# Four converted weight units parked in DRAM after their first use, instead of converted a second time

## The chip, the cores and the metric

The kernel runs on one core of a Trainium2 chip. The metric is device time in microseconds of one execution, as the median of three runs. TensorE (PE) multiplies matrices, PEld loads its weights, VectorE (DVE), ScalarE (ACT) and GpSimd (POOL) do the elementwise work, and SyncE (SP) issues nearly all the transfers, in order, on one queue. TensorE has a granted clock, which the profile prints as a share of full speed.

## The reference, cut to what matters

```
x = attention(rope(q), rope(k), v)        # 2 batches x 8 heads, 576 rows of 64 -> x: 1152 tokens x 512
h = x @ w_in                              # 512 -> 2048      w_in, w_out are float64
g = max(0.01 * h, h)
x1 = (g @ w_out).astype(float32)          # 2048 -> 512
# then a mixture of 8 experts, top 2 of 8 per token:
for e: out[rows of e] += gate * (relu(x1[rows of e] @ w1[e]) @ w2[e])
```

Only the middle part, `x1`, has weights in double precision. Everything else is float32.

## The kernel before, in words

The kernel has three stages: attention (to about 180 us of the span), the dense feed-forward layer (to about 400 us) and the experts.

Every product is made in split precision: a float32 value is written as a high part and a low part, each in a type that TensorE multiplies at full rate, and three products (high-high, low-high, high-low) are added. So each weight has to be converted before TensorE can use it.

**Units and slots.** The 2048 hidden features are 16 units of 128. A unit has two parts, its slice of `w_in` (part 0) and of `w_out` (part 1), 0.5 MB of float64 each. Its converted form is two tiles of 128x2x512 (`hi`, `lo`), 0.5 MB each, in one of `NSLOT` = 12 slots (line 143). The list `units` (lines 149, 150) runs c = 0..15 for the 16 dense units, c = 16..19 for the first four of them again, and c = 20 on for the expert units. Unit c lives in slot c % 12, so c = 12..15 overwrite units 0..3, and 16..19 overwrite 4..7. Slots 1 and 2 share their memory with the last set of q and k of the attention stage (`set_q`, `set_k`).

**Two passes.** The dense layer handles the first 768 tokens in one pass over c = 0..15 (lines 641 to 649) and the last 384 in `dense2` (line 662) over c = 4..19: the twelve units that are still in slots, and then the four that have been overwritten.

**Conversion of a dense part** (`convert`, line 179) is a chain of six stages on 128x512 elements: ACT takes the absolute value (0), DVE clamps (1), shifts and takes in the sign (2, two instructions), takes in the low word (3), ACT writes `hi` (4), DVE writes `lo` (5). Part p = 2c or 2c + 1. An expert part is float32 and needs stages 4 and 5 only. `load_part` (line 153) brings a raw part into one of three buffers.

**Order.** PE, ACT, DVE and POOL run their instructions in the order in which the program writes them. In attention that order is a string of letters; in the dense layer `leaky` (line 588), called once per step, weaves its own activation (`g_t`, `g_f`, `g_h`, `g_l`), the conversion stages of parts p - 1, p, p + 1, and the hooks, which hold the routing of the first 768 tokens and the copies of `x1` rows to DRAM (`rows`, line 715). `dense2` converts parts 32 on, two per unit. The transfers are put in order on SP's queue by a scheduler, which works from the dependences.

**Closing a head pair.** In attention the softmax sums of each pair go to DRAM (`inv_sums`, line 464), come back to all partitions (`inv_sum`, line 470), POOL multiplies (line 474) and ACT writes `xh` (line 486). All these transfers are on SP's queue.

Of the kernel before, what the change touches and what calls it, by code (L numbers as in the profile page):

```python
# [10 lines left out]
F32 = mybir.dt.float32  # L11
# [66 lines left out]
def f32(t):  # L78
    return t.bitcast(F32)
# [3 lines left out]
def fused_kernel(ctx, tc, q, k, v, w_in, w_out, w_gate, w_noise, noise, w1, w2, consts, out):  # L83
    nc = tc.nc
    V, A, G, T = nc.vector, nc.scalar, nc.gpsimd, nc.tensor

    def pool(name, bufs=1, **kw):
        return tc.tile_pool(name=name, bufs=bufs, reuse_waits="tile", **kw)
# [9 lines left out]
    dpool = ctx.enter_context(pool("scratch", space=DRAM))  # L98
# [44 lines left out]
    NSLOT = 12  # L143
    slots = [[epool.tile([128, 2, 512], F32R, name=f"w{n}_0") for n in "hl"]]
# [5 lines left out]
    units += [("ex", e, f) for e in range(E) for f in range(8)]  # L150
    staged = {}

    def load_part(p):

        c, part = divmod(p, 2)
        if p >= last_part[0] or p in staged or (p, 0) in done:
            return
        u = units[c]
        if u[0] == "in":
            f = u[1]  # L160
            t = rpool.tile([128, 512, 2], I32, name="raw")
            if part == 0:
                nc.sync.dma_start(t.rearrange("p (k f) w -> p k (f w)", k=4),
                                  w_in.bitcast(I32)[:, f * 256:(f + 1) * 256].rearrange("(k p) f -> p k f", p=128))
            else:
                nc.sync.dma_start(t.rearrange("p d w -> p (d w)"), w_out.bitcast(I32)[f * 128:(f + 1) * 128, :])
        else:
            _, e, f = u
            t = rpool.tile([128, 512], F32, name="raw32", tag="raw")
            if part == 0:  # L170
                nc.sync.dma_start(t.rearrange("p (k f) -> p k f", k=4),
                                  w1[e, :, f * 128:(f + 1) * 128].rearrange("(k p) f -> p k f", p=128))
            else:
                nc.sync.dma_start(t, w2[e, f * 128:(f + 1) * 128, :])
        staged[p] = t

    word, done, last_part, last_conv = {}, set(), [2 * len(units)], [2 * len(units)]

    def convert(p, stage):

        c, part = divmod(p, 2)
        if not 0 <= p < last_conv[0] or (p, stage) in done:
            return
        done.add((p, stage))
        hi, lo = slots[c % NSLOT]
        if units[c][0] == "in":
            if stage == 0:
                word[p] = rpool.tile([128, 512], I32, name="word")
                A.activation(f32(word[p]), f32(staged[p][:, :, 1]), AF.Abs)
                return  # L190
            m, hw, lw = word[p], staged[p][:, :, 1], staged[p][:, :, 0]
            if stage == 1:
                V.tensor_scalar(f32(m), f32(m), 2.0 ** -15, F32_MAX_AS_HIGH_WORD, op0=OP.max, op1=OP.min)
            elif stage == 2:
                V.tensor_scalar(m, m, 3, 0x3FFFFFFF, op0=OP.logical_shift_left, op1=OP.bitwise_and)
                V.scalar_tensor_tensor(m, hw, -0x40000000, m, op0=OP.bitwise_and, op1=OP.bitwise_or)
            elif stage == 3:
                V.scalar_tensor_tensor(m, lw, 29, m, op0=OP.logical_shift_right, op1=OP.bitwise_or)
            elif stage == 4:
                A.activation(hi[:, part], f32(m), AF.Copy)  # L200
            else:
                V.tensor_tensor(lo[:, part], f32(m), f32(hi)[:, part], op=OP.subtract)
        else:
            t = staged[p]
            if stage == 4:
                A.activation(hi[:, part], t, AF.Copy)  # L206
            elif stage == 5:
                V.tensor_tensor(lo[:, part], t, f32(hi)[:, part], op=OP.subtract)  # L208
# [279 lines left out]
    def x_low(pr):  # L488
        k, parts = x_parts(pr)
        t = closing.pop(pr)[4]  # L490
        for i, there, here in parts:
# [41 lines left out]
            "t": (sums, [(pr, n) for pr in range(NP) for n in range(3)]),  # L533
            "B": (sums_in, [(pr, n) for pr in range(NP) for n in range(2)]),
            "Z": (load_small, [(i,) for i in range(7)]), "F": (load_part, [(p,) for p in range(6)])}
    for n, f in (("T", invert), ("s", sums_out), ("N", normalize), ("X", x_high), ("Y", x_low)):
        work[n] = (f, [(pr,) for pr in range(NP)])
# [4 lines left out]
    for i, n in enumerate("!#$%&*"):  # L542
        work[n] = (convert, [(p, i) for p in range(6)])
# [26 lines left out]
    def mm1(c, h, x, cols, n, lows_last=False):  # L570
        hi, lo = slots[c % NSLOT]
        terms = [(k, w, m) for k in range(4) for w, m in ((hi, x[0]), (lo, x[0]), (hi, x[1]))]
        if lows_last:
            terms.sort(key=lambda t: t[2] is x[1])
        for i, (k, w, m) in enumerate(terms):
            T.matmul(h[:, :n], w[:, 0, k * 128:(k + 1) * 128], m[:, k, cols:cols + n], start=(i == 0), stop=(i == 11))  # L576

    def mm2(c, g, y, n, first, last):

        hi, lo = slots[c % NSLOT]  # L580
        for d in range(4):
            ds = slice(d * 128, d * 128 + 128)
            b, o, opens = y[d]
            for t, (w, m) in enumerate(((hi, g[0]), (lo, g[0]), (hi, g[1]))):
                T.matmul(b[:, o:o + n], w[:, 1, ds], m[:, :n], start=(first and opens and t == 0),  # L585
                         stop=(last and t == 2), skip_group_check=True)

    def leaky(h, n, ps, hooks, group):

        t = gpool.tile([128, 512], F32, name="g_t")  # L590
        g = gpool.tile([128, 512], F32, name="g_f")
        gh = gpool.tile([128, group], F32R, name=f"g_h{group}")
        gl = gpool.tile([128, group], F32R, name=f"g_l{group}")
        for at, p in enumerate(ps):
            convert(p, 1)
            if at == 0:
                A.activation(t[:, :n], h[:, :n], AF.Copy, scale=0.01)  # L597
                V.tensor_tensor(g[:, :n], h[:, :n], t[:, :n], op=OP.max)  # L598
            if at < len(hooks):
                hook(hooks[at])  # L600
            convert(p - 1, 4)
            convert(p, 2)
            if at == 0:
                A.activation(gh[:, :n], g[:, :n], AF.Copy)
                V.tensor_tensor(gl[:, :n], g[:, :n], f32(gh)[:, :n], op=OP.subtract)  # L605
            convert(p, 3)
            convert(p - 1, 5)
            convert(p + 1, 0)
            load_part(p + 3)
        return gh, gl  # L610
# [6 lines left out]
    for p in (6, 7, 8):  # L617
        load_part(p)
# [14 lines left out]
    def step(c, o, n):  # L633
        h = hA if o == 0 else hB
        mm1(c, h, x, o, n)
        q = next(calls)
        return leaky(h, n, (6 + q,), (base + q,), NA if o == 0 else NB)
# [3 lines left out]
    for f in range(17):  # L641
        if f < 15:
            gA[f + 1] = step(f + 1, 0, NA)
        if f < 16:
            mm2(f, gA.pop(f), ya, NA, f == 0, f == 15)
        if f > 0:
            gB[f - 1] = step(f - 1, NA, NB)
        if f > 1:
            mm2(f - 2, gB.pop(f - 2), yb, NB, f == 2, False)
# [6 lines left out]
    def close_first():  # L656
        mm2(15, gB.pop(15), yb, NB, False, True)
        for n in range(2):
            e = A.copy if n else V.tensor_copy
            e(x1[0][:, 2 * n:2 * n + 2, NA:P1], bank[4 + n].rearrange("p (d n) -> p d n", d=2))  # L660

    def dense2(cs, p, at):

        x = (xh[1], xl[1])
        g = None
        for i in range(len(cs) + 1):
            if i < len(cs):
                h = bank[6 + i % 2]
                mm1(cs[i], h, x, 0, NC)
                after = leaky(h, NC, (p + 2 * i, p + 2 * i + 1), (at + 2 * i, at + 2 * i + 1), NA)  # L670
            if i == 0:
                close_first()
            else:
                mm2(cs[i - 1], g, ya, NC, i == 1, i == len(cs))
            g = after
        for d in range(4):
            (A.copy if d % 2 else V.tensor_copy)(x1[0][:, d, P1:NT], bank[d][:, :NC])
# [234 lines left out]
    last_part[0], last_conv[0] = 2 * len(units), 58  # L912
    load_part(32)
    dense2(list(range(16 - NSLOT, 16 + 16 - NSLOT)), 28, base2)
    assert not later, later.keys()

# [221 lines left out]
```

## Time and profile before

| | us |
|---|---|
| median of three runs (lowest to highest) | 676.95 (676.53 to 681.25) |
| the profiled execution | 678.88 |
| its span, first to last instruction | 677.1 |
| PE busy | 645.0 (95%) |
| DVE busy | 418.7 (62%) |
| ACT busy | 325.7 (48%) |
| POOL busy | 173.5 (26%) |

The mean granted clock is 0.981. PE is busy almost all of the span, so shares over the span say little; the stretches in which PE waits, or runs at a lower clock, are few, and the windows of 10 us show where they are. A row of the timeline is one instruction or a merged run of them: start, duration, engine, line, operation, output <- inputs, shape, count, and in brackets how long the engine stood idle before it and what ended that.

### The profile page before, as it was taken

How to read it: one execution, taken by the hardware profiler on the slowest of the kernel's cores; microseconds unless marked ns; L12 is line 12 of the kernel's file. 1: busy time of each engine (PE TensorE's matmuls, PEld its weight loads, DVE VectorE, ACT ScalarE, POOL GpSimd, SP SyncE). 2: the span in 40 equal slices, each digit the busy share in tenths (PEclk: the TensorE clock that was granted, in tenths of full speed). 3: DMA queues.
4: the chain of work that ended last, by engine and by line, in shares of the span. 5: the costliest groups of instructions: out<-in, count | busy, mean ns of one | idle time of the engine just before them, and what ended most of it. 6: DMA issues, size and time to landing. Idle time of an engine off the chain costs nothing. (4 is left out here: it accounts for less than half of the span.)

```text
span 677.1 us, 10441 instructions
## 1 busy us (share of the span) xinstructions
PE 645.0 (95%) x3658; PEld 555.9 (82%) x3659; DVE 418.7 (62%) x870; ACT 325.7 (48%) x659; POOL 173.5 (26%) x179
## 2 busy tenths in 40 slices
PE   7698999999999999999979998999999999999993
PEld 3587888888788888889769985889888888888882
DVE  8688555564179988843598654474756556574611
ACT  4454555575445544423445441454555545454511
POOL 9974767112130000000000001113224040505102
PEclk9899999999999999999998997999999999999998
DMA  6656433231147443420154433447676675858323
GB/s 173 188 166 180 116 75 76 63 80 51 36 139 263 147 124 125 125 63 1 56 163 140 133 92 80 134 134 194 155 201 162 196 171 165 215 148 204 103 31 41
DMA packets 89344, 86.51 MB, mean 128 GB/s; under 512 B 21316, under 2 KB 68615, under 8 KB 89287
## 3 DMA queue, kind: packets, MB, share of 16 engines
q1 hardware_dynamic: 84390, 74.92, 38.3%
q0 software_dynamic: 4608, 10.49, 7.7%
q8 instruction: 30, 0.49, 0.3%
q10 hardware_dynamic: 288, 0.39, 0.2%
q14 instruction: 28, 0.22, 0.1%
HBM read 69.95 MB, written 10.00 MB: 118 GB/s over the span
## 5 line engine op out<-in xcount | busy, mean ns | idle before, releaser
L208 DVE TENSOR_TENSOR wl<-raw,wh 128x512 fp32r<-128x512 f32 x108 | 72.3, 687 | 48.9 <-ACT wh L206 45.9
L999 POOL DMA_INDIRECT out<-y_row,idx x24 | 41.9, 1744 | 174.6 <-ACT y_row L991 170.3
L873 POOL DMA_INDIRECT got<-x_rows,idx x24 | 25.0, 1043 | 227.6 <-DVE gate L825 210.3
L206 ACT ACTIVATE wh<-raw 128x512 fp32r<-128x512 f32 x108 | 66.0, 629 | 32.9 <-DMA raw<-in_moe_w 32.4
L374 DVE TENSOR_REDUCE maxes<-pM 128x1 fp32r<-128x576 f32 (+1 forms) x73 | 54.1, 754 | 44.0 <-PE pM L367 43.4
L982 PE MATMUL bank<-wh,g_x 128*128 128x512 f32 x216 | 78.3, 403 | 0.6 <-ACT set_q L206 0.5
L436 PE MATMUL pO<-p,VF 128*128 128x288 f32 x256 | 72.7, 413 | 0.0
L423 ACT ACTIVATE p<-pS 128x576 f32<-128x576 f32 (+1 forms) x73 | 46.3, 649 | 53.0 <-PE pS L417 51.3
L576 PE MATMUL bank<-xe_h,wh 128*128 128x320 f32 x216 | 67.8, 314 | 0.0
L576 PE MATMUL bank<-xe_h,wl 128*128 128x320 f32 x216 | 67.7, 314 | 0.0
L576 PE MATMUL bank<-xe_l,wh 128*128 128x320 f32 x216 | 66.8, 312 | 0.0
L597 ACT ACTIVATE g_t<-bank 128x512 f32<-128x512 f32 (+2 forms) x48 | 23.5, 489 | 75.9 <-PE bank L576 75.9
L585 PE MATMUL bank<-g_l,wh 128*128 128x384 f32 (+2 forms) x152 | 52.1, 342 | 0.9 <-DVE g_l L605 0.9
L436 PEld LDWEIGHTS pO<-p,VF 128*128 128x128 f32 x256 | 45.2, 192 | 8.9 <-issue 1.1
L585 PE MATMUL bank<-g_h,wh 128*128 128x384 f32 (+2 forms) x152 | 52.4, 345 | 0.0
L576 PE MATMUL bank<-xh,wh 128*128 128x384 f32 (+2 forms) x152 | 52.1, 343 | 0.0
L576 PE MATMUL bank<-xh,wl 128*128 128x384 f32 (+2 forms) x152 | 51.9, 342 | 0.0
L576 PE MATMUL bank<-xl,wh 128*128 128x384 f32 (+2 forms) x152 | 51.8, 341 | 0.0
L585 PE MATMUL bank<-g_h,wl 128*128 128x384 f32 (+2 forms) x152 | 51.6, 339 | 0.0
L598 DVE TENSOR_TENSOR g_f<-bank,g_t 128x512 f32<-128x512 f32 (+2 forms) x48 | 26.6, 555 | 38.9 <-ACT g_t L597 38.6
L965 DVE SCALAR_TENSOR_TENSOR g_x<-bank,g_x 128x320 fp32r<-128x320 f32 x64 | 31.0, 484 | 30.1 <-ACT g_x L964 30.0
L982 PEld LDWEIGHTS bank<-wh,g_x 128*128 128x128 f32 x216 | 40.5, 188 | 8.4 <-ACT set_q L206 0.8
(238 smaller groups left out, 1530.4 us busy)
## 6 DMA issues: line engine op xcount, KB each, us to landing
raw<-in_moe_w SPq DMA_DIRECT2D x128, 256.0 KB
raw<-in_moe_w_in SPq DMA_DIRECT2D x20, 512.0 KB
raw<-in_moe_w_out SPq DMA_DIRECT2D x20, 512.0 KB
inv_sum<-inv_sums SPq DMA_DIRECT2D x16, 144.0 KB
out<-none SPq DMA_DIRECT2D x9, 256.0 KB
raw_q<-in_q SPq DMA_DIRECT2D x8, 256.0 KB
raw_k<-in_k SPq DMA_DIRECT2D x8, 256.0 KB
VF<-in_v SPq DMA_DIRECT2D x16, 128.0 KB
```

Source lines behind the costliest of these rows:

```text
L206: A.activation(hi[:, part], t, AF.Copy)
L208: V.tensor_tensor(lo[:, part], t, f32(hi)[:, part], op=OP.subtract)
L374: V.tensor_reduce(maxes[pr % 2][rows, i:i + 1], maxed.pop((pr, a, j))[rows, :, 0:288], axis=AX.XY, op=OP.max, negate=True)
L423: A.activation(t[r], scored.pop((pr, a, j))[r, :, 0:288], AF.Exp, scale=0.125)
L436: T.matmul(acc[g][:, z, 0:288], w, p[r, z, :], start=opens, stop=closes)
L576: T.matmul(h[:, :n], w[:, 0, k * 128:(k + 1) * 128], m[:, k, cols:cols + n], start=(i == 0), stop=(i == 11))
L585: T.matmul(b[:, o:o + n], w[:, 1, ds], m[:, :n], start=(first and opens and t == 0), stop=(last and t == 2), skip_group_check=True)
L598: V.tensor_tensor(g[:, :n], h[:, :n], t[:, :n], op=OP.max)
L873: G.indirect_dma_start(out=t[:n], out_offset=None, in_=x1_rows, in_offset=bass.IndirectOffsetOnAxis(ap=idx[e][:n, st:st + 1], axis=0))
L965: V.scalar_tensor_tensor(g[:, C:2 * C], h[:, :C], 0.0, f32(g)[:, :C], op0=OP.max, op1=OP.subtract)
L982: T.matmul(yr[st], s, w, start=(f == 0 and t == 0), stop=(f == 7 and t == 2))
L999: s = G.indirect_dma_start(out=out, out_offset=bass.IndirectOffsetOnAxis(ap=idx[e][:n, st:st + 1], axis=0), in_=r[:n], in_offset=None, com ...
```

## The change: four units are written out and read back

When the first pass has reached f = 3..6, the converted `hi` and `lo` of units 0..3 are written to DRAM (`keep`). In `dense2`, after the last product with unit c - 12, they are read into the slot of unit c = 16..19 (`bring`). Raw loads and conversions of c = 16..19 are left out.

```diff
+    def keep(c, w):
+        kept[c, w] = dpool.tile([128, 1024], F32, name=f"kept{c}_{w}", bufs=1)
+        nc.sync.dma_start(kept[c, w], f32(slots[c % NSLOT][w]).rearrange("p a b -> p (a b)"))
+
+    def bring(c, w):
+        nc.sync.dma_start(f32(slots[c % NSLOT][w]).rearrange("p a b -> p (a b)"), kept[c - 16, w])
     def load_part(p):
-        if p >= last_part[0] or p in staged or (p, 0) in done:
+        if p >= last_part[0] or p in staged or (p, 0) in done or 16 <= c < 32 - NSLOT:
             return
     def convert(p, stage):
-        if not 0 <= p < last_conv[0] or (p, stage) in done:
+        if not 0 <= p < last_conv[0] or (p, stage) in done or 16 <= c < 32 - NSLOT:
             return
     ...
             mm2(f, gA.pop(f), ya, NA, f == 0, f == 15)
+        if 3 <= f < 19 - NSLOT:
+            for w in range(2):
+                keep(f - 3, w)
     ...
                 mm2(cs[i - 1], g, ya, NC, i == 1, i == len(cs))
+                c = cs[i - 1] + NSLOT
+                if c < 32 - NSLOT:
+                    for w in range(2):
+                        bring(c, w)
```

The orders of PE and POOL stay as they are. DVE loses 40 instructions and ACT 16, all of them the conversion of parts 32 to 39; SP loses eight loads and gains eight stores and eight loads, and the scheduler puts them in places that the diff does not show.

On DVE, in `dense2` around the fourth to the sixth of its units (`word` is the part under conversion, `noisy`, `mx`, `ix` belong to the routing), before:

```order
L193 TENSOR_SCALAR word<-word 128x512
L598 TENSOR_TENSOR g_f<-bank_1893,g_t 128x384
L769 TENSOR_TENSOR noisy<-c,ln 128x48
...
L777 MAX_INDEX ix<-mx,noisy 128x8 x6
L195 TENSOR_SCALAR word<-word 128x512
L196 SCALAR_TENSOR_TENSOR word<-raw,word 128x512
L605 TENSOR_TENSOR g_l_3533<-g_f,g_h_3532 128x384
L198 SCALAR_TENSOR_TENSOR word<-raw,word 128x512
L202 TENSOR_TENSOR wl_1881<-word,wh_1880 128x512
```

and with the change:

```order
L608 TENSOR_TENSOR g_f<-bank_1893,g_t 128x384
L786 TENSOR_TENSOR noisy<-c,ln 128x48
...
L794 MAX_INDEX ix<-mx,noisy 128x8 x6
L615 TENSOR_TENSOR g_l_3493<-g_f,g_h_3492 128x384
L608 TENSOR_TENSOR g_f<-bank_1892,g_t 128x384
```

The activation and the routing keep their order, and the conversions between them are gone.

On SP, in attention, around the closing of the first head pair (`wh_88`, `wl_89` are slot 0; `raw<-in_moe_w_out` and `raw<-in_moe_w_in` are parts 5 and 6), before:

```order
L270 DMA raw_k_116<-in_k 128x2x256
L273 DMA raw_k_116<-in_k 64x2x64
L464 DMA inv_sums<-rc 128x9
L166 DMA raw<-in_moe_w_out 128x1024
L470 DMA inv_sum<-inv_sums 64x576 x2
L163 DMA raw<-in_moe_w_in 128x4x256
```

and with the change:

```order
L158 DMA kept_0_2187<-wh_88 128x1024
L280 DMA raw_k_116<-in_k 128x2x256
L176 DMA raw<-in_moe_w_out 128x1024
L474 DMA inv_sums<-rc 128x9
L283 DMA raw_k_116<-in_k 64x2x64
L158 DMA kept_1_2189<-wl_89 128x1024
L173 DMA raw<-in_moe_w_in 128x4x256
L480 DMA inv_sum<-inv_sums 64x576 x2
```

The two stores of unit 0 are issued here, not in the dense layer, and two loads of raw weights have moved ahead of the sums. The stores of unit 1 stand in the same way just ahead of `inv_sums` of the sixth pair, those of unit 2 behind it, and those of unit 3 at the start of the dense layer.

On SP, in `dense2`, with the change (`raw_3462`, `raw_3516`, `raw_3526`, `raw_3570` are the first four expert parts):

```order
L181 DMA raw_3462<-in_moe_w 128x4x128
L184 DMA raw_3516<-in_moe_w 128x512
L181 DMA raw_3526<-in_moe_w 128x4x128
L161 DMA wl_1877<-kept_1_2189 128x1024
...
L161 DMA wl_1883<-kept_1_2453 128x1024
L743 DMA x_rows<-x_row 128x512
L161 DMA wh_1882<-kept_0_2451 128x1024
L743 DMA x_rows<-x_row 128x512 x2
L184 DMA raw_3570<-in_moe_w 128x512
```

Before, five loads of dense parts stood between the first rows of `x1` here; now the first three expert parts come first, then the eight loads from DRAM.

## Rows read from the trace of the kernel before

**Rows 1.** Windows: busy time of each engine, granted clock, DMA share, GB/s.

```profile
210.00:220.00 10.00, 10.00 (x57) 8.71 (x56) 9.67 (x21) 5.60 (x11) 0.00 (x0) 1.00 0.76 263
340.00:350.00 10.00, 8.78 (x53) 8.46 (x52) 9.69 (x22) 5.66 (x11) 0.00 (x0) 1.00 0.68 199
350.00:360.00 10.00, 6.89 (x27) 6.26 (x26) 9.69 (x40) 3.29 (x8) 0.00 (x0) 0.70 0.34 102
360.00:370.00 10.00, 10.00 (x64) 9.91 (x63) 8.63 (x29) 6.89 (x14) 0.00 (x0) 0.95 0.50 148
```

**Rows 2.** Timeline of PE in dense2: start, duration, instruction, idle before.

```profile
337.60 0.33 PE L576 MATMUL bank<-xh,wh 128*128 128x384 f32 x1
342.24 0.33 PE L576 MATMUL bank<-xh,wh 128*128 128x384 f32 x1
345.72 0.66 PE L718 MATMUL bank<-ct,x 128*128 128x128 f32 x4 [1.23 <-ACT x_row L720]
352.77 0.66 PE L718 MATMUL bank<-ct,x 128*128 128x128 f32 x4 [2.21 <-ACT x_row L720]
354.67 0.69 PE L585 MATMUL bank<-g_l,wh 128*128 128x384 f32 x1 [0.90 <-DVE g_l L605]
358.04 0.52 PE L576 MATMUL bank<-xh,wh 128*128 128x384 f32 x1
363.96 0.33 PE L576 MATMUL bank<-xh,wh 128*128 128x384 f32 x1
```

**Rows 3.** Timeline of ACT in the same stretch.

```profile
352.15 0.56 ACT L720 COPY x_row<-bank 128x512 f32<-128x512 f32 x1
```

**Rows 4.** DVE by line, 326 to 362 us: count, busy us, mean ns.

```profile
L196 DVE SCALAR_TENSOR_TENSOR word<-raw,word 128x512 int32<-128x512 int32 x8 | 5.5, 693 | 0.3
L198 DVE SCALAR_TENSOR_TENSOR word<-raw,word 128x512 int32<-128x512 int32 x8 | 5.5, 688 | 0.1
L202 DVE TENSOR_TENSOR wl<-word,wh 128x512 fp32r<-128x512 f32 x8 | 5.5, 684 | 0.0
L195 DVE TENSOR_SCALAR word<-word 128x512 int32<-128x512 int32 x8 | 3.4, 421 | 0.1
L193 DVE TENSOR_SCALAR word<-word 128x512 f32<-128x512 f32 x8 | 3.4, 420 | 1.1 <-ACT word L189 1.1
```

**Rows 5.** Windows in attention, and one in the dense layer; columns as in Rows 1.

```profile
56.00:60.00 4.00, 4.00 (x26) 3.57 (x25) 3.93 (x9) 1.30 (x2) 1.15 (x1) 1.00 0.45 89
60.00:64.00 4.00, 4.00 (x26) 3.47 (x25) 3.93 (x8) 1.94 (x4) 0.00 (x0) 1.00 0.81 224
64.00:68.00 4.00, 4.00 (x26) 3.52 (x26) 1.43 (x3) 2.51 (x5) 1.83 (x2) 1.00 0.87 274
208.00:212.00 4.00, 4.00 (x21) 3.35 (x20) 3.97 (x10) 2.19 (x5) 0.00 (x0) 1.00 1.07 399
```

**Rows 6.** Timeline of SP's queue in attention.

```profile
59.63 1.12 SPq L470 DMA_DIRECT2D inv_sum<-inv_sums  x2
...
152.98 0.33 SPq L464 DMA_DIRECT2D inv_sums<-rc  x1
```

**Rows 7.** Timeline of POOL in attention.

```profile
65.22 1.41 POOL L474 TENSOR_TENSOR inv_sum<-unnorm,inv_sum 128x576 f32<-128x576 f32 x1 [8.07 <-DMA raw<-in_moe_w_in]
...
158.01 1.92 POOL L474 TENSOR_TENSOR inv_sum<-unnorm,inv_sum 128x576 f32<-128x576 f32 x1 [14.89 <-DMA inv_sum<-inv_sums]
```

**Rows 8.** Timeline of ACT in attention and in the first dense pass.

```profile
66.83 0.68 ACT L486 ACTIVATE xh<-inv_sum 128x576 fp32r<-128x576 f32 x1
67.73 1.32 ACT L330 ACTIVATE TQ<-pT 64x576 fp32r<-64x576 f32 x2 [0.23 <-PE pT L321]
...
161.98 0.77 ACT L486 ACTIVATE xh<-inv_sum 128x192 fp32r<-128x192 f32 x2
...
214.61 0.68 ACT L189 ACTIVATE word<-raw 128x512 f32<-128x512 f32 x1 [1.72 <-DMA raw<-in_moe_w_out]
```

**Rows 9.** Timeline of DVE in attention.

```profile
150.87 0.69 DVE L202 TENSOR_TENSOR set_q<-word,set_q 128x512 fp32r<-128x512 f32 x1 [0.29 <-ACT set_q L200]
```

More of the change, by code (lines that the diff above doesn't have):

```diff
@@ L151, in fused_kernel @@
     staged = {}
+    kept = {}
+    def keep(c, w):
[3 more added lines that the diff above has]
+        nc.sync.dma_start(f32(slots[c % NSLOT][w]).rearrange("p a b -> p (a b)"), kept[c - 16, w])
     def load_part(p):
         c, part = divmod(p, 2)
-        if p >= last_part[0] or p in staged or (p, 0) in done:
+        if p >= last_part[0] or p in staged or (p, 0) in done or 16 <= c < 32 - NSLOT:
             return
```

## The prediction

> **What bounds the kernel now.** I read the windows first. PE is busy nearly everywhere, so only a stretch in which PE waits or is slowed can give time back. In the dense layer there is one such stretch: PE is busy 8.78 us of 340 to 350 and 6.89 of 350 to 360, its granted clock falls to 0.70 and is 0.95 in the next ten, while DVE is busy 9.69 of 10 in both [rows 1]. DVE, not PE, sets the pace there.
>
> Next the timeline of PE. One unit of `dense2` with one transposed row takes 342.24 - 337.60 = 4.64 us when nothing is late. From then on PE stands idle 1.23, 2.21 and 0.90 us, and the three units from 342.24 to 363.96 take 21.72 us [rows 2]. Three times 4.64 is 13.92, so **7.80 us are lost**: 4.34 idle, and 3.46 in which PE multiplies slowly (matmuls of 0.52 us at 358.04 against 0.33). The waits name ACT's row copy twice and DVE's `g_l` once. ACT is no bottleneck; it is busy 5.66 and 3.29 us in these windows [rows 1]. Its copy at 352.15 [rows 3] stands in its queue behind the `hi` stage of a conversion, which has to wait for DVE. So all three waits lead back to DVE.
>
> Then DVE by line. Parts 32 to 39 cost it five instructions each, 40 in all, with 5.5 + 5.5 + 5.5 + 3.4 + 3.4 = 23.3 us busy between 326 and 362 [rows 4]. Those are exactly the ones that the change removes.
>
> **What it removes.** Spread over those 36 us, 13 of DVE's 19.4 us from 340 to 360 go, so it is busy a third of the time, and ACT's copies have nothing ahead of them that waits for a conversion. I take the whole 7.80 us. The slow clock goes with the idle time that stands before it; if it stayed, only 4.34 would come. Removed loads and ACT instructions give nothing of their own: ACT has room, and the loads were waiting for DVE.
>
> **Reading back.** Eight loads of 0.52 MB must land before unit 16 starts, the 13th of `dense2`. The last may start once unit 7's products are done, at 342.24 at the latest [rows 2]. At the lower of the two busy rates in attention, 224 GB/s [rows 5], all eight take 4.19 MB / 224 = 18.7 us, so they would be there by 361 even if none had started earlier, before the unit that starts at 363.96, and four further units run before the 13th. Price 0. SP waits for PE at each of these loads, and behind them stand row copies, which are needed after `dense2`, and the fourth expert part, whose buffer is not free before that. The first three expert parts have moved ahead. Price 0, and if that cover went, a late expert load would stop DVE and then PE in the way that rows 2 show.
>
> **Writing out** is where the change pays. T is the time of one store of 0.52 MB. No store of this kind is in the trace; the bounds are 1.3 us, at the 399 GB/s of the window in which the zeros are written to the output, and 2.3 us, at 224 GB/s among loads [rows 5].
>
> Unit 0's stores go out at about 55 and 59 us, ahead of the read-back of the first pair's sums. That read-back was issued at 59.63 [rows 6], and POOL got it only at 65.22 [rows 7]: the transfers were already backed up, at a DMA share of 0.81 and 0.87 [rows 5]. POOL ended at 66.63 and ACT's `xh` started at 66.83 [rows 7, 8], so there is no slack on that way. Behind it ACT turns the next pair's q and k for PE; there ACT had waited 0.23 us for PE [rows 8], and that is all the room. The first store falls into 56 to 60, where DMA is busy 0.45 of the time [rows 5], which leaves a hole of 2.2 us, and is free. The second delays the sums by T, so PE stops for T - 0.23: 1.1 us at the lower bound, 2.1 at the upper. I take 1.1, since a store in rows of 4 KB is nearest to the writing of zeros.
>
> The Trainium skill (DMA: Bandwidth & Descriptors, section on queues, rings and completion order) says that each DMA engine consumes its ring's descriptors in ring order, which speaks against the change: a small urgent transfer pays for every large one ahead of it. Its ceiling of 435 GB/s (Specifications) would make T an estimated 1.2 us, and the loss 1.0 instead of 1.1.
>
> Unit 1's stores stand ahead of the sixth pair's sums. Its `lo` is ready at 150.87 + 0.69 = 151.56 [rows 9], and the sums are issued at 152.98 [rows 6]. If both stores started only then, they would delay the sums by 2T - 1.42. POOL was done at 159.93 and ACT needed it at 161.98 [rows 7, 8], a slack of 2.05. So the price is 2T - 3.47 if positive: 0 at 1.3 us, 1.1 at 2.3. I take 0, as the first goes earlier. Unit 2's stores come after these sums; what stands behind them serves the next closing, half a pair later: 0.
>
> Unit 3's stores fall together with the zeros and the loads of the first dense pass. A load already came 1.72 us late to ACT there [rows 8], and PE did not stop, 10.00 of 10 [rows 1]. One or two more stores add 1.3 to 2.6 us to that. I take 0 and bound it by 0.9, by which 2.6 exceeds the lateness that PE has already stood.
>
> **Sum.** -7.8 + 1.1 = -6.7 us. The profiled execution of 678.88 us would take 672.2. The median of the runs is 676.95, 1.93 less, since the profiled one is a single run in a spread of 676.53 to 681.25; on it the forecast is **670.2 us**, 0.99% faster. One per cent, about what a measurement can tell from no change, is 6.8 us, so the forecast lies on that line, and the uncertain costs decide the side.
>
> **Rivals.**
> *Attention hides the stores.* If the second store ends before the sums' store is answered, nothing is lost: 676.95 - 7.8 = 669.2. For it: PE is busy all of 60 to 68 us although POOL waits [rows 5, 7], so it may have more room than ACT's 0.23 us. Against: POOL's 8.07 us wait [rows 7].
>
> *Both waits are paid in full, and the clock falls with them.* At T = 2.3 the loss is 2.1 + 1.1 = 3.2, so 672.4 without the clock. In the window with 1.22 us of idle the clock stayed at 1.00 (2.4 GHz), in the next, with 3.11, it went to 0.70 of it, part of it at the lower level [rows 1]. Should the stop in attention end like the second, the clock would take some 3.5 us more, as it did in `dense2`: -7.8 + 3.2 + 3.5 = -1.1, so 675.9. The Trainium skill (TensorE: Matmul & The Clock Gate, Part 1) says that idle throttles the array to half its clock, and the trace agrees at 350 us.
>
> *The stores are slow, and the kernel is slower than before.* The mechanism is the same queue: with T above 2.2 the hole is full, the first pair loses 2T - 2.43, the sixth 2T - 3.47, together 4T - 5.9. This eats the 7.8 us from T = 3.4 us on (153 GB/s), and makes the kernel slower by over 1% from T = 5.2 (102 GB/s). At T = 6 it would give 676.95 - 7.8 + 18.1 = 687. For it: no row shows such a store. Against: zeros and loads together move 399 GB/s.
>
> *DVE's work is not what PE waits for* and only the 3.46 us of clock or the 4.34 us of idle come back: 672.6 to 673.5, or 673.7 to 674.6 with the store's 1.1. Against: DVE's 9.69 in both windows.
>
> **How the numbers follow.** Forecast (T from 1.0 to 2.0, 669.9 to 671.0) 0.50; stores hidden 0.24; waits in full 0.09, with the clock 0.04 more; only part of the gain 0.08; slow stores 0.05. The range takes the first two, the waits in full without the clock, and most of the partial gain: 668.7 (0.5 below the best case, for the spread of runs) to 674.0. Left out are the slow stores, the clock case and the end of the partial gain, some 0.12. Faster by over 1% means under 670.2: the hidden case and two fifths of the forecast, 0.24 + 0.20 = 0.44. Slower by over 1% needs T over 5.2, 0.03. The rest, 0.53, is within 1%.
>
> **What would show it.** The windows from 340 to 370 with PE at 10 and clock 1.00, and units of 4.64 us there; DVE under 6 of 10; PE idle near 68 to 73 us with a release that leads to `inv_sum`, about 1 us; POOL's product of the first pair (line 474, 484 in the new numbering) later than 65.22; no wait of PE for the loads from DRAM. It is wrong if PE still waits for ACT's row copies, if the clock still falls near 350, if a load of raw weights late near 215 stops PE, or if POOL gets the first sums no later than before.

## The result, and the profile after

| | before | with the change |
|---|---|---|
| median of the runs, us (lowest to highest, number) | 679.47 (676.13 to 683.63, 12) | 673.60 (671.02 to 678.46, 12) |
| ratio to before, 95% interval | | 0.9917 (0.9895 to 0.9939) |
| the profiled execution, us | 678.88 | 673.01 |
| its span, us | 677.1 | 670.9 |

By the ratio the change makes the kernel 0.83% faster, about 5.6 us. The forecast was 0.99%, 6.7 us, and 670.2 us with a range of 668.7 to 674.0.

**dense2** did what the forecast says. The windows of the kernel after, columns as in [rows 1]:

```profile
210.00:220.00 10.00, 10.00 (x57) 8.69 (x56) 8.07 (x17) 4.61 (x9) 0.00 (x0) 1.00 0.93 339
340.00:350.00 10.00, 10.00 (x62) 9.92 (x61) 4.50 (x29) 2.98 (x6) 0.00 (x0) 1.00 0.82 281
350.00:360.00 10.00, 10.00 (x62) 9.92 (x61) 6.00 (x22) 4.66 (x10) 0.00 (x0) 1.00 0.25 81
360.00:370.00 10.00, 10.00 (x66) 9.95 (x65) 6.69 (x19) 5.28 (x11) 0.00 (x0) 1.00 0.58 159
```

PE is at 10 of 10 where it stood at 8.78 and 6.89, its clock at 1.00 where it fell to 0.70, and DVE has fallen from 9.69 to 4.50 and 6.00. In the timeline of PE after, the transposes of the rows, two of which had waited [rows 2], now come without a wait:

```profile
341.63 0.60 PE L735 MATMUL bank<-ct,x 128*128 128x128 f32 x4
346.27 0.60 PE L735 MATMUL bank<-ct,x 128*128 128x128 f32 x4
350.91 0.60 PE L735 MATMUL bank<-ct,x 128*128 128x128 f32 x4
355.55 0.60 PE L735 MATMUL bank<-ct,x 128*128 128x128 f32 x4
360.19 0.60 PE L735 MATMUL bank<-ct,x 128*128 128x128 f32 x4
```

They are 4.64 us apart, each of them, which is the forecast's unit with nothing late.

**Attention** lost more than forecast. Here are the three engines on the way of the first pair's sums. SP's queue after:

```profile
54.39 0.59 SPq L158 DMA_DIRECT2D kept<-wh  x1
...
57.22 0.34 SPq L176 DMA_DIRECT2D raw<-in_moe_w_out  x1
57.68 0.36 SPq L474 DMA_DIRECT2D inv_sums<-rc  x1
...
58.78 0.59 SPq L158 DMA_DIRECT2D kept<-wl  x1
60.08 0.38 SPq L173 DMA_DIRECT2D raw<-in_moe_w_in  x1
60.88 1.13 SPq L480 DMA_DIRECT2D inv_sum<-inv_sums  x2
```

POOL's product and the engine that needs it, ACT, after:

```profile
67.32 1.41 POOL L484 TENSOR_TENSOR inv_sum<-unnorm,inv_sum 128x576 f32<-128x576 f32 x1 [10.68 <-DMA inv_sum<-inv_sums]
```

```profile
68.76 0.69 ACT L496 ACTIVATE xh<-inv_sum 128x576 fp32r<-128x576 f32 x1 [2.29 <-POOL inv_sum L484]
...
71.21 0.25 ACT L406 ACTIVATE mr<-pR 5x128 fp32r<-5x128 f32 x1
```

And PE after, from the turning of the fourth pair's k on, with the first matmul of the dense layer, the first of the routing behind the first pass, and the last of the dense layer:

```profile
67.34 0.71 PE L331 MATMUL pT<-ct,rope_k 128*128 128x128 f32 x5
71.52 1.56 PE L427 MATMUL pS<-set_q,set_k 128*128 128x288 f32 x8 [1.41 <-ACT mr L406]
...
182.08 0.61 PE L586 MATMUL bank<-xh,wh 128*128 128x512 f32 x1
...
322.56 1.89 PE L720 MATMUL bank<-x,wgn 128*16 128x512 f32 x4
...
394.48 0.34 PE L595 MATMUL bank<-g_l,wh 128*128 128x384 f32 x1
```

The same points in the kernel before, first SP, then PE:

```profile
58.18 0.35 SPq L464 DMA_DIRECT2D inv_sums<-rc  x1
```

```profile
67.81 0.71 PE L321 MATMUL pT<-ct,rope_k 128*128 128x128 f32 x5
70.19 1.44 PE L417 MATMUL pS<-set_q,set_k 128*128 128x288 f32 x8
...
180.29 0.61 PE L576 MATMUL bank<-xh,wh 128*128 128x512 f32 x1
...
320.62 3.61 PE L703 MATMUL bank<-x,wgn 128*16 128x512 f32 x8
...
400.36 0.34 PE L585 MATMUL bank<-g_l,wh 128*128 128x384 f32 x1
```

POOL waits for the read-back, ACT for POOL (2.29 us, where it had not waited at all [rows 8]), and PE stands 1.41 us for ACT's `mr`, which is queued behind that `xh`. The group that stood starts 4.18 us after the turning of the fourth pair's k, where it was 2.38 before: 1.80 us later. Single executions differ by some us in their first 50, so I compare stretches inside a run, and use the same three for every experiment:

- **sums' way**: from SP's issue of the first pair's `inv_sums` to POOL's product; before 65.22 - 58.18 = 7.04, after 67.32 - 57.68 = 9.64
- **attention**: from the turning of the fourth pair's k (the expectations below count the pairs from 0 there and call it the third) to the first dense matmul; before 180.29 - 67.81 = 112.48, after 182.08 - 67.34 = 114.74
- **dense2**: from the first routing matmul to the last dense one; before 400.36 - 320.62 = 79.74, after 394.48 - 322.56 = 71.92

So dense2 gives 7.82 us, attention takes 2.26 (1.80 at the stop, the rest in small pieces behind it), and the sum is -5.56. That agrees with the 5.6 of the runs; the two profiled spans differ by 6.2, the rest of which lies outside these stretches.

### The profile page after: what moved, and what is told of

It is laid out like the page before. It is cut to its first block, busy times and chain, and to the rows that moved or that the text cites. A ratio compares the mean times of both kernels' runs of the same rounds, so it can differ in the third digit from the quotient of the medians.

```text
span 670.9 us, 10384 instructions
## 1 busy us (share of the span) xinstructions
PE 639.8 (95%) x3655; PEld 551.3 (82%) x3659; DVE 398.3 (59%) x830; ACT 317.0 (47%) x643; POOL 170.3 (25%) x179
## 5 line engine op out<-in xcount | busy, mean ns | idle before, releaser
L890 POOL DMA_INDIRECT got<-x_rows,idx x24 | 23.6, 985 | 216.5 <-DVE gate L842 199.8
```

The lines of the kernel that those rows point to most:

```text
L890: G.indirect_dma_start(out=t[:n], out_offset=None, in_=x1_rows, in_offset=bass.IndirectOffsetOnAxis(ap=idx[e][:n, st:st + 1], axis=0))
```

## The experiments

| kernel | ratio to before (95%) | median | sums' way | attention | dense2 |
|---|---|---|---|---|---|
| before | | 679.5 | 7.04 | 112.48 | 79.74 |
| the change | 0.9917 (0.9895 to 0.9939) | 673.6 | 9.64 | 114.74 | 71.92 |
| the change again | 0.9929 (0.9905 to 0.9954) | 675.1 | 9.99 | 115.04 | 71.93 |
| all stores late | 0.9888 (0.9862 to 0.9913) | 671.7 | 7.10 | 112.63 | 71.93 |
| unit 0's stores late | 0.9901 (0.9873 to 0.9928) | 672.7 | 7.11 | 112.51 | 71.93 |
| stores alone | 1.0036 (1.0017 to 1.0055) | 682.1 | 10.27 | 115.63 | 81.28 |
| unit 0's second store late | 0.9882 (0.9858 to 0.9906) | 671.4 | 8.23 | 112.89 | 71.92 |
| part 6 behind | 0.9913 (0.9890 to 0.9935) | 674.3 | 7.14 | 113.75 | 71.93 |
| part 6 far behind | 0.9906 (0.9874 to 0.9938) | 673.0 | 8.04 | 112.73 | 71.92 |
| second store twice | 0.9963 (0.9945 to 0.9981) | 676.3 | 9.92 | 113.49 | 71.93 |
| the same, second profile | (one run) | 676.8 | 11.66 | 119.73 | 71.95 |
| sums on POOL's queue | 0.9957 (0.9934 to 0.9981) | 677.4 | 9.78 | 117.15 | 71.95 |
| two units kept | 0.9884 (0.9856 to 0.9913) | 671.2 | 7.18 | 112.61 | 72.48 |

The median of before, measured beside each series, was 679.2 to 679.8.

**The change again.** No edit.

> The changed kernel once more, beside the others of this series, as their measure. If the first comparison holds: 5.6 us below the kernel before (ratio about 0.992), first dense matmul near 182.1 us (before 180.3), POOL's first-pair product near 67.3 us, dense2 without a stop. If the 1.8 us lost in attention were only the scatter of single runs, the first dense matmul would fall anywhere between 179.8 and 182.3 here.

Ratio 0.9929, sums' way 9.99, attention 115.04. The loss in attention repeats (2.56 us) and is no scatter.

**All stores late.** The stores go out on ACT's queue, whose order is the program's.

```diff
-        nc.sync.dma_start(kept[c, w], f32(slots[c % NSLOT][w])...)
+        nc.scalar.dma_start(kept[c, w], f32(slots[c % NSLOT][w])...)
```

> All eight stores are issued from ACT's queue in the first dense pass, at the place where the program writes them, and no longer by SP in attention. Theory A (the stores of unit 0, ahead of the first pair's sums, are the whole loss): first dense matmul back at 180.3 us, POOL's first-pair product near 65.2, no new stop of PE in 180 to 320 us, dense2 still 7.8 us shorter, so about 7.6 us below the kernel before (ratio near 0.989) and 1.8 below the change. Rival C (the stores cost wherever they run, by what they take from the other transfers, or the issuing holds ACT up): the loss moves into the dense pass, PE stops there by 1 to 2 us, and the time stays 5.6 us below the kernel before.

Theory A's numbers came: sums' way 7.10, attention 112.63, dense2 71.93, ratio 0.9888. In the dense pass the stores share DMA with the loads, and PE does not notice. Windows of this kernel:

```profile
210.00:220.00 10.00, 10.00 (x57) 8.68 (x56) 9.53 (x21) 5.93 (x12) 0.00 (x0) 1.00 0.97 339
220.00:230.00 10.00, 10.00 (x57) 8.72 (x56) 9.81 (x20) 5.94 (x12) 0.00 (x0) 1.00 0.90 341
230.00:240.00 10.00, 10.00 (x61) 8.87 (x61) 8.83 (x18) 4.85 (x9) 0.00 (x0) 1.00 0.83 296
```

(The first dense matmul itself stood at 182.38 us, not at 180.3: this run was late from its start on. That is why the stretches are used.)

**Only unit 0 late.**

```diff
+        (nc.sync if c else nc.scalar).dma_start(kept[c, w], ...)
```

> Only the two stores of unit 0 go from ACT's queue in the first dense pass; those of units 1 to 3 stay on SP's queue where the change has them. The forecast's price for units 1 to 3 is 0: the time from the third pair's turning of k on PE to the first dense matmul is 112.5 us as in the kernel before (114.7 and 115.0 with the change), and the whole is as fast as with all eight late, ratio near 0.9885. If units 1 to 3 cost what their upper bounds say (1.1 for the sixth pair, 0.9 at the start of the dense pass): up to 2 us slower than that, ratio near 0.991.

Attention 112.51, the same as before. The six stores of units 1 to 3 cost nothing there, as forecast. The ratio of 0.9901 holds 0.9885 in its interval.

**Stores alone.** `bring` and the two conditions on 16 <= c are taken out.

> The eight stores stay as in the change, but nothing is read back: the four units are loaded and converted a second time as in the kernel before, so DVE has its 40 instructions again. If the two parts of the sum are independent: first dense matmul near 182.1 us as with the change, the stop in dense2 back (PE 6.9 of 10 us from 350 to 360, shifted by 1.8), so 1.8 to 2.0 us slower than the kernel before (ratio about 1.003). The forecast's own figure for the stores was 1.1 us (ratio 1.0016). If the stall in dense2 was partly of another origin, this kernel would be no slower than the kernel before.

Ratio 1.0036, 2.4 us slower than before, attention +3.15. With the 40 conversions back, the stop in dense2 is back. PE of this kernel:

```profile
350.52 0.66 PE L731 MATMUL bank<-ct,x 128*128 128x128 f32 x4 [1.23 <-ACT x_row L733]
357.58 0.66 PE L731 MATMUL bank<-ct,x 128*128 128x128 f32 x4 [2.20 <-ACT x_row L733]
...
366.13 0.66 PE L731 MATMUL bank<-ct,x 128*128 128x128 f32 x4 [2.54 <-ACT x_row L733]
```

The first two are the waits of [rows 2], within 0.01 us. The third has no counterpart in the kernel before; with it dense2 is 1.5 us longer than before in this profile, which is the slowest execution of its runs, 685.6. So the gain hangs on the conversions and not on the stores. By the ratio the whole kernel loses 2.4 us (1.2 to 3.7), about twice the 1.1 us that was forecast for the stores, but a part of it may be that third wait.

**The second store of unit 0 late.**

```diff
+        (nc.scalar if (c, w) == (0, 1) else nc.sync).dma_start(kept[c, w], ...)
```

> Only the second store of unit 0 (its low part) is moved to ACT's queue in the first dense pass; the first store and the load of part 6 stay ahead of the first pair's read-back, as the change has them. The forecast's reading (the first store falls into a hole, the second is the whole loss): POOL's first-pair product back at 65.2 us, first dense matmul at 180.3, 1.8 us below the change. Theory A with both stores counting: about half comes back, POOL near 66, first dense matmul near 181.2. Rival B (the load of part 6, which moved ahead of the read-back, is the loss): next to nothing comes back, POOL near 67, first dense matmul near 182.

Sums' way 8.23, attention 112.89. SP's rows of this kernel, then POOL's:

```profile
56.73 0.36 SPq L474 DMA_DIRECT2D inv_sums<-rc  x1
...
60.21 1.11 SPq L480 DMA_DIRECT2D inv_sum<-inv_sums  x2
```

```profile
64.96 1.40 POOL L484 TENSOR_TENSOR inv_sum<-unnorm,inv_sum 128x576 f32<-128x576 f32 x1 [10.02 <-DMA inv_sum<-inv_sums]
```

Of the loss of 2.26 only 0.41 stays. That is nearly the outcome that the forecast's reading asks for, but the way of the sums is still 1.2 us longer than before, so something else had been added too. At this point the load of part 6 was the suspect.

**Part 6 behind the read-back.** Both stores stay in attention.

```diff
+    (nc.scalar if p == 6 else nc.sync).dma_start(...)     # in load_part
     # in x_high, behind ACT's xh
+        if pr == 0:
+            load_part(6)
```

> The change with one edit: the load of part 6 (0.5 MB of raw w_in), which the scheduler had moved ahead of the first pair's read-back, is issued from ACT's queue behind ACT's first-pair output instead. Both stores stay where they are. Rival B (part of the loss is this moved load and not a store): from the sums' issue to POOL's product 8.4 to 8.8 us instead of 9.6 to 10.0, about 1.2 us of the loss of 2.3 to 2.6 gone, ratio near 0.9905. Theory A with the first store counting: 9.6 to 10.0 us as in the change, ratio near 0.9925.

Sums' way 7.14, less than either theory's number: with both stores ahead of it, the read-back reaches POOL as early as in the kernel before. SP's rows of this kernel, then POOL's:

```profile
56.33 1.08 SPq L158 DMA_DIRECT2D kept<-wh  x1
...
59.73 0.34 SPq L176 DMA_DIRECT2D raw<-in_moe_w_out  x1
60.20 0.36 SPq L474 DMA_DIRECT2D inv_sums<-rc  x1
...
61.29 0.59 SPq L158 DMA_DIRECT2D kept<-wl  x1
63.43 1.11 SPq L480 DMA_DIRECT2D inv_sum<-inv_sums  x2
```

```profile
67.34 1.42 POOL L484 TENSOR_TENSOR inv_sum<-unnorm,inv_sum 128x576 f32<-128x576 f32 x1 [8.18 <-ACT p L433]
```

The profile puts POOL's wait down to ACT's `p` here, but the product does not read `p`. By the semaphore times in the trace the read-back landed at 67.18 us, when `p` ended too, so the two came together, and POOL could not have started earlier without the read-back. Attention still took 1.27 us more than before: PE now waits for the move of the next k, which the load of part 6, put where it now was, seems to have held up. PE of this kernel:

```profile
75.58 0.50 PE L377 MATMUL pM<-TK,TQ 128*128 128x288 f32 x2 [0.92 <-DMA TK<-TK]
```

**Part 6 far behind.** The same with `pr == 1`.

> Both stores of unit 0 stay ahead of the first pair's read-back, as in the change; the load of part 6 goes from ACT's queue behind ACT's output of the second pair (some 10 us later than in the last such run, where it held back the move of the next k and PE stood 0.92 us for that). Theory B (what delays the first pair is the load of part 6, moved ahead of the read-back; one store in its place costs no more than the raw load that stands there in the kernel before): from the sums' issue to POOL's product 7.1 us, no stop of PE, from the third pair's turning of k to the first dense matmul 112.5 us, and the whole as fast as with all stores late, ratio near 0.989. Theory A (a store ahead of the sums costs its own time): 8.4 us or more and a stop of over 0.8 us there, ratio near 0.991.

Attention 112.73 and no stop of PE behind the turning of the fourth pair's k, though both stores stand where the change put them. The sums' way is 8.04 us, between the two theories, but POOL's product is early enough for ACT. The ratio of 0.9906 has the 0.989 in its interval; a small part of what is missing may be that PE now waits 0.40 and 0.17 us at 197 us, for the last pair's `xh` and `xl`.

**The second store twice.**

```diff
+        if (c, w) == (0, 1):
+            again = dpool.tile([128, 1024], F32, name="again", bufs=1)
+            nc.sync.dma_start(again, f32(slots[c % NSLOT][w])...)
```

> The change with one more store: the low part of unit 0 is written to DRAM twice, the second time right behind the first, ahead of the first pair's read-back. From the issue of the first pair's sums to POOL's product it is 7.0 us in the kernel before and 9.6 and 10.0 in two runs of the change, and with the low part's store taken away 8.2. Theory A (a store ahead of the read-back delays it by its own T, now put at 1.4 to 1.8 us): 11.0 to 11.8 us here, PE stands still that much longer, so 1.4 to 1.8 us above the change, ratio to the kernel before about 0.995. If T were the upper bound of 2.3: 12.2 us. Rival (the read-back waits for something else, such as the buffer of the raw load ahead of it, and a store is hidden behind that): 9.6 to 10.0 and ratio about 0.9925.

The profile showed the rival's number, 9.92, but the runs went the way of theory A and further, 2.3 to 3.1 us above the change by the ratios where 1.4 to 1.8 were expected. The profiled execution stood at the low end of its runs (674.5 of 674.3 to 678.8), and TensorE was slow in it ahead of the wait (a group of eight matmuls took 2.12 us at 58.36, 1.22 in the second profile). So a second profile was taken.

> The kernel with the doubled second store once more, for a second profile: the first shows the sums' way at 9.92 us, no longer than with one store, but its runs are 2.5 to 3 us slower than those of the change. If the profiled run was typical: 9.9 us again and the third pair's turning of k to the first dense matmul 113.5 to 115 us. If it was an exception (TensorE was slow from 56 to 61 us in it, ahead of the wait): 11 us or more, and 116 us or more.

11.66 us: a further store adds 11.66 - 9.64 = 2.0 or 11.66 - 9.99 = 1.7. PE of this second profile, then its windows:

```profile
67.03 0.71 PE L334 MATMUL pT<-ct,rope_k 128*128 128x128 f32 x5
73.25 2.29 PE L430 MATMUL pS<-set_q,set_k 128*128 128x288 f32 x8 [3.46 <-ACT mr L409]
```

```profile
66.00:72.00 6.00, 3.79 (x23) 2.82 (x21) 0.76 (x1) 1.64 (x4) 2.15 (x2) 1.00 0.54 124
72.00:78.00 6.00, 4.75 (x16) 4.18 (x17) 3.04 (x5) 3.63 (x7) 5.92 (x6) 0.51 0.43 99
```

PE stands 3.46 us, and the granted clock from 72 to 78 us is 0.51, the lower of its two levels. The group of eight matmuls takes 2.29 us instead of 1.56. This is the forecast's rival in which the clock falls with the wait. The Trainium skill (TensorE: Matmul & The Clock Gate, Part 1) says that idle halves the clock; this row agrees, and the 1.41 us stop of the change, with 1.00 in the windows from 60 to 78, did not bring it. Attention costs 7.25 us here, with 2 us more delay than in the change. Why the first profile kept the sums' way at 9.92 stays open.

**The sums on POOL's queue.**

```diff
-        nc.sync.dma_start(u[3]...)              # sums_out, and sums_in alike
+        (nc.sync if pr else nc.gpsimd).dma_start(u[3]...)
```

> The change with the first pair's sums sent to DRAM and read back from POOL's queue, which has nothing else in it then; stores and raw loads stay on SP's queue where the change has them. If the first pair waits because its three small transfers stand in line behind large ones of the same queue: from the sums' issue to POOL's product below 6 us, no stop of PE, ratio near 0.989. If it waits because the transfers that run at the same time share the bandwidth of the DMA engines (0.9 to 1.0 busy there): 8 to 10 us as in the change, the stop of 1.4 us or more stays, ratio 0.992 or above.

Sums' way 9.78, as in the change, and the stop stays. POOL of this kernel:

```profile
62.28 0.76 POOL L474 DMA_DIRECT2D inv_sums<-rc  x1 [1.33 <-DVE rc L469]
66.94 1.10 POOL L480 DMA_DIRECT2D inv_sum<-inv_sums  x2 [3.90 <-DMA inv_sums<-rc]
72.06 1.40 POOL L484 TENSOR_TENSOR inv_sum<-unnorm,inv_sum 128x576 f32<-128x576 f32 x1 [4.02 <-DMA inv_sum<-inv_sums]
```

In a queue with nothing ahead of it, 4.5 KB of sums took 66.94 - 62.28 = 4.66 us to be known in DRAM, longer than in SP's queue of the change (60.88 - 57.68 = 3.20); the read-back then took 72.06 - 66.94 = 5.12 to reach POOL instead of 67.32 - 60.88 = 6.44. So taking the sums out of SP's line does not bring them earlier. The prediction had leaned on the queue's order. The Trainium skill (DMA: Bandwidth & Descriptors, section "Issuing engines are not separate DMA queues") says that transfers of every issuing engine share the same DMA engines and interleave, and this run, with its 9.78 us, agrees as far as it goes. But the profile lists POOL's queue as another kind, software_dynamic where SP's is hardware_dynamic, and how long the sums take on it with nothing beside them was not measured. A part of the 4.66 may be that queue's own, so this run doesn't show by itself that the transfers running at the same time are what makes the sums late. PE lost 0.45 us at 85.9 and 1.28 at 95.2 as well.

**Two units kept.**

```diff
-        if p >= last_part[0] ... or 16 <= c < 32 - NSLOT:
+        if p >= last_part[0] ... or 18 <= c < 32 - NSLOT:
-        if 3 <= f < 19 - NSLOT:
+        if 5 <= f < 19 - NSLOT:
     ...                                        # the same in convert, and in the condition on bring
```

> Only units 2 and 3 are written out and read back; units 0 and 1 (parts 32 to 35) are loaded and converted a second time as in the kernel before, so DVE keeps 20 of the 40 instructions, 11.6 us, and no store stands ahead of the sums of the first or the sixth pair. Theory A (what stops PE in dense2 is the queue that builds up in front of DVE where conversions and the routing meet, about 340 to 360 us; parts 32 to 35 are through by then): no stop there, 7.8 us back, no loss in attention, ratio near 0.9885. Rival (the stop goes with DVE's total work, so half of the conversions bring half): 3 to 4.5 us of the 7.8 stay lost, the clock falls below 0.9 in 350 to 360, ratio 0.993 to 0.995.

Theory A holds nearly whole: dense2 takes 72.48 us, 7.26 less than before, with half of the conversions still there. Windows and PE of this kernel:

```profile
340.00:350.00 10.00, 9.67 (x59) 9.31 (x58) 9.65 (x34) 5.60 (x11) 0.00 (x0) 1.00 0.86 262
350.00:360.00 10.00, 10.00 (x62) 9.93 (x62) 5.86 (x30) 4.66 (x10) 0.00 (x0) 1.00 0.45 157
```

```profile
347.59 0.66 PE L735 MATMUL bank<-ct,x 128*128 128x128 f32 x4 [0.33 <-ACT x_row L737]
```

DVE is just as full as before from 340 to 350 (9.65), but has caught up by 350, and PE waits once, for 0.33 us. Attention costs nothing, since units 0 and 1 are not stored. With four of the eight stores, this is as fast as the best of the others.

**The best versions.** All stores late, the second store late, and two units kept, at 0.9882 to 0.9888, lie below the change, and each other's intervals hold them. Their intervals still overlap that of the change (0.9895 to 0.9939), so the runs alone hardly separate them from it; the attention stretch does, with 112.61 to 112.89 against 114.74 and 115.04.

## Why the prediction was right in its mechanism and off in one term

**dense2: right, to 0.02 us.** The forecast took 7.80, idle and slow clock together; 7.82 came, from one profile of the kernel before. Stores alone brought the stop back, and two units kept removed nearly all of it with half of the conversions, which ties it to the conversions around 340 to 360 us. The rival by which only a part comes back fell. One number on the way was off: of DVE's 19.4 us from 340 to 360 some 8.9 went and not 13, so it is busy half of the time and not a third; no price hung on it.

**Reading back: right.** No wait of PE on `kept`, and the units keep their 4.64 us.

**Units 1, 2 and 3: right at 0.** POOL ended the sixth pair's product at 161.37 + 1.41 = 162.78, where it was 159.93 [rows 7]. Of these 2.85 us, 1.79 are the later arrival of this run at the dense layer (182.08 against 180.29), so the stores delay it by 1.1, and the slack of 2.05 covers that. (The prediction's 2T - 1.42 gives 1.2 at T = 1.3.) PE did not stop, in the windows of the kernel after:

```profile
150.00:160.00 10.00, 10.00 (x61) 8.83 (x60) 8.73 (x16) 6.38 (x12) 0.00 (x0) 1.00 0.56 174
160.00:170.00 10.00, 10.00 (x57) 8.63 (x56) 2.71 (x4) 6.10 (x12) 2.96 (x3) 1.00 0.46 164
```

At the start of the dense pass ACT waited 3.32 us for a raw load instead of 1.72 [rows 8], in ACT's timeline after:

```profile
217.65 0.67 ACT L199 ACTIVATE word<-raw 128x512 f32<-128x512 f32 x1 [3.32 <-DMA raw<-in_moe_w_out]
```

That is within the 1.3 to 2.6 us that the prediction added to it, and PE stayed at 10.00 in 210 to 220.

**Unit 0's store: the term that was mis-sized.** The step was "the second delays the sums by T, so PE stops for T - 0.23: 1.1 us". PE lost 2.26 and 2.56. Its second half holds: the sums' way grew by 2.60 and 2.95 us, so the room was 0.3 to 0.4 where 0.23 stood (0.8 in "second store late", 1.19 against 0.41). The rival by which attention hides the stores fell with it. What failed is the delay, which is not one store. The scheduler also moved two raw loads of 0.5 MB: part 5 to just ahead of the sums, and part 6 ahead of their read-back. The order shown ahead of the prediction has both, and the prediction put no price on either.

The way has two legs, and both grew. From the issue of the sums to that of their read-back it is 59.63 - 58.18 = 1.45 us before [rows 6] and 3.20 after; from there to POOL 65.22 - 59.63 = 5.59 before [rows 6, 7] and 67.32 - 60.88 = 6.44 after. The first leg is just as long when the second store is taken away (60.21 - 56.73 = 3.48) or the load of part 6 (63.43 - 60.20 = 3.23), so neither of these two makes it long. In the three kernels that keep unit 0's stores out of attention it is 1.44 or 1.45. What those with the long leg share is the first store and the load of part 5 ahead of the sums, the latter issued 0.46 us ahead of them in the change; no run moved part 5 alone back, so it is not shown which of the two does it. The second leg falls from 6.44 to 64.96 - 60.21 = 4.75 and 67.34 - 63.43 = 3.91 when one of the two is taken away.

With one large transfer between the issues of the sums and of their read-back (a raw load in the kernel before, the store in "part 6 behind" and "far behind", the load in "second store late") the way takes 7.04 to 8.23 us; with two, 9.64 to 10.27; with three, 11.66 in one profile and 9.92 in another. Taking either of the two away brings nearly the whole loss back (attention 112.89 and 112.73): what then remains of the delay, 1.19 and 1.00 us, costs PE only 0.41 and 0.25. So the delay of 2.6 comes of the second store and the moved loads together, and the loss can't be given to one of them.

T itself is not one number: 1.4 to 1.8 us by taking the second store away, 1.7 to 2.0 by the second profile of doubling it, which are between its bounds of 1.3 and 2.3, but 0.3 or nothing by the first profile; and with part 6 out of the way both stores together add only 0.1 to 1.0. A store that costs 3.4 us or more was not seen. (In that rival a loss of 1% begins at T = 5.1, not 5.2.)

**The clock in attention** did not fall in the change. One more store brought it down in one profile of two, so the rival was about one transfer away.

**The base.** 670.2 was counted from a median of three, 676.95; over twelve runs of the same kernel it is 679.47. Of the 3.4 us between 670.2 and 673.6, 2.5 are this, and the rest is about what the store's term lacks. Both errors go the same way, and 673.6 lies only 0.4 inside the range, which had been drawn for other cases; that the time still fell into it is in part luck. The prediction set the profiled execution's 678.88 aside as the odd one; it was the typical one. A difference carries over, an absolute time does not.

## What to carry to other kernels

When work is moved to a queue that a scheduler fills, price every large transfer that changes its place around the small urgent one, not only the new ones: list what stands right ahead of it and between its two legs, before and after. A stage that is held up by a backlog gets all its time back when the backlog fits, and half of the relief can be enough; so do the cheapest half first. Where an early store has no hurry, issue it from a queue whose order is the program's, at a place where the transfers have room.

## What the runs showed of the hardware

- A small transfer among large ones was no earlier on another queue: the sums took 9.64 and 9.99 us to POOL's product on SP's queue, 9.78 on POOL's (whose own time with nothing beside it was not measured).
- A stop of 1.41 us left the granted clock at 1.00 in the windows around it, one of 3.46 us, which ended at 73.25, had 0.51 from 72 to 78.
- Executions of one kernel differ by some 7 us, and the profiles differ by 6 us within the first 50 already: the turning of the third pair's k starts between 44.2 and 50.3 us in the thirteen, and their granted clock from 20 to 40 us is 0.66 to 0.91. Stretches inside a run agree much better: dense2 is 71.92 to 71.95 in ten profiles of eight kernels.
